# One transpose per query tile in place of two: one-hots and weight columns share a tile

## The chip, the cores and the metric

The kernel runs on one core of a Trainium2 chip. The metric is the device time of one launch in microseconds (us), taken in several runs; the median counts. One further execution is recorded by the hardware profiler, instruction by instruction. Its engines are TensorE (PE for matmuls, PEld for the loading of their stationary operand), VectorE (DVE), ScalarE (ACT), GpSimd (POOL) and the DMA queues, of which SP is the one that matters here.

## The reference

Causal attention of 8 batches, 12 heads, 448 positions and head size 64 makes an array x of 3584 tokens by 768. A gate then sends each token to one of 8 experts, and each expert keeps the 80 tokens of largest gate weight:

```python
attn = softmax(mask(q @ k.T / 8));  x = (attn @ v) as (3584, 768)
logits = x @ w_gate;  expert_idx = argmax(logits, 1)
gate_w = softmax(logits)[arange(N), expert_idx]
for e in range(8):
    tok = where(expert_idx == e)
    if len(tok) > 80: tok = the 80 of largest gate_w
    out[tok] = gate_w[tok] * (relu(x[tok] @ w1[e]) @ w2[e])   # other rows stay 0
```

## The kernel before

The program has two stages. The attention stage goes over 48 pairs of heads, six pairs to a batch. Behind it comes the expert stage, which gathers 80 tokens per expert and streams the expert weights. Between the two lies a tail, whose order is written out by hand (`TAIL`).

Each pair takes eight slots, and each engine gets its instructions in the order in which the slots issue them and executes them in that order. In the pair with number i, TensorE makes the scores of pair i + 1 at the end of slot 7, turns the probabilities of pair i - 1 in four groups of transposes (`TSLOT`: group 0 in slot 0, groups 1 and 2 in slot 1, group 3 in slot 4; tiles `tp`), and multiplies pair i - 2 with the values in slot 5 (`xp`, line 619). VectorE shifts the scores (line 558, tiles `ns`, seven shifts in slots 0, 0, 1, 2, 3, 4, 4, of widths 192, 192, 320, 320, 448, 448, 64). ScalarE takes the exponential (line 562) and copies groups 0 to 2 of the transposed probabilities to SBUF (line 601, tiles `PT`); group 3 is copied by VectorE in slot 5. Within a slot the order of issue is: group transposes, values, shifts, copies, exponential, and then the planned steps of the routing.

The routing of a batch is a list of named steps with a slot number each, counted from the end of the batch's own pairs (`STEPS`; for batch 6, the last but one, `EARLY`; batch 7, the last, takes its order from `TAIL`). Thus the steps of batch b run while the pairs of batch b + 1 are worked on, and slot 41 is slot 1 of that batch's sixth pair. The steps that matter here:

- `columns` and `parts` (GpSimd, in the last batch VectorE and GpSimd): they write one-hots of the chosen expert, three copies side by side, into the tile `oh3` (the profile calls it `oh`), and five groups of eight columns into the tile `mv`: two for the token's number and three for its gate weight, split into three bf16 parts.
- `r0t` and `r1t` (TensorE, line 864, tile `selt`): four transposes each, one per query tile of 128 tokens, of the one-hots (`r0t`) and of the weight columns (`r1t`), into a PSUM bank each.
- `r0c` and `r1c` (VectorE, line 867): copies of the 24 rows that count, to the halves 0 and 1 of the SBUF tile `ex`.
- `rl` (TensorE, line 894): reads half 0 of `ex` and compares with the table of the batches before; there is none for batch 0. `lt` (line 900) reads its result on VectorE.
- `c3w` to `c0w` (TensorE, line 878, tiles `rn`): read both halves; `c3l` to `c0l` (VectorE, line 881, `less`).

Row groups (`rt`, line 730, scaled on VectorE at line 749 into `xr`) turn the finished tokens back; in batches 0 to 5 one of them is turned in slot 40, in batch 6 one each in slots 35 and 36.

PSUM tiles of the pool `ps_g` go round through four banks in the order of issue, so a tile waits until the tile four places before it has been read. Its takers are `tp`, `selt`, `rt`, `rn`, `rl`, `xp` and some others.

Of the kernel before, what the change touches and what calls it, by code (L numbers as in the profile page):

```python
# [17 lines left out]
P = 128  # L18
# [8 lines left out]
NORMS = [0, 2, 4]  # L27
ROWS0 = [(2, 2), (3, 4), (9, 9), (19, 20)]
ROWS1 = [(27, 28), (35, 36), (36, 38), (40, 41)]
STEPS = {'gp': 20, 'gs': 22, 'lp': 24, 'lg': 25, 'logit': 26, 'shifted': 27, 'chosen': 32, 'sums': 33, 'one_hot': 33, 'columns': 33, 'weight': 35, 'weighted': 36, 'parts': 37, 'r0t': 41, 'r0c': 42, 'r1t': 42, 'r1c': 43, 'rl': 44, 'lt': 46, 'c3w': 49, 'c3l': 50, 'cp': 52, 'ro': 52, 'places': 54, 'c2w': 56, 'c2l': 57, 'places2': 54, 'c1w': 58, 'c1l': 59, 'c0w': 59, 'c0l': 60, 'earlier': 60, 'gt': 65, 'own': 67, 'rank': 67, 'rr': 68, 'tn': 73, 'tab': 74, 'rp': 76, 'row': 78}  # L30
EARLY = {'gp': 18, 'gs': 20, 'lp': 24, 'lg': 25, 'logit': 26, 'shifted': 26, 'chosen': 28, 'sums': 29, 'one_hot': 29, 'columns': 29, 'weight': 30, 'weighted': 30, 'parts': 30, 'r0t': 33, 'r0c': 34, 'r1t': 35, 'r1c': 36, 'rl': 36, 'lt': 38, 'c3w': 40, 'c3l': 41, 'c2w': 41, 'c2l': 42, 'c1w': 42, 'c1l': 43, 'cp': 43, 'ro': 43, 'c0w': 44, 'c0l': 45, 'earlier': 45, 'places': 46, 'places2': 46, 'gt': 46, 'own': 47, 'rank': 47, 'rr': 47, 'tn': 49, 'tab': 49, 'rp': 52, 'row': 53}
THIRD = [0, 0, 2, 2, 4, 6, 8]
THIRD_EARLY = [0, 2, 4, 6, 6, 8, 9]
EARLY_GATE = (2, 3)
# [138 lines left out]
def attention_then_moe(  # L173
# [12 lines left out]
    nc = tc.nc  # L186
    B, _, NP, S = qT.shape
    N, D = out.shape
    E = wg.shape[2]
# [3 lines left out]
    NT = (S + P - 1) // P  # L193
# [50 lines left out]
    SL = max(2, min(P, CAP))  # L244
    NSL = (CAP + SL - 1) // SL
    NV = 5

    COUNT = F16 if CAP + S <= 2048 else F32
    ZR = 4
# [4 lines left out]
    OFF, at = {}, 0  # L254
# [49 lines left out]
    for e, which in LAYERS:  # L304
# [4 lines left out]
        k = (K1, K2)[which - 1]  # L309
# [42 lines left out]
        return [lambda j=j, x=x: load_chunk(*got[0], j, x, 2) for j in range(k) for x in range(2)]  # L352


    mv = one_hots = mv_flat = oh_flat = expert_cols = tables = table_rows = None
# [4 lines left out]
    lg = keep.tile([P, NT, (H + 1) * E], F32, name="lg")  # L360
# [35 lines left out]
    def late_constants():  # L396


        def padded(shape, name):
            t = spool.tile(shape, BF16, name=name, tag=name, bufs=1)  # L400
            nc.gpsimd.memset(t, 0.0)
            return t
# [20 lines left out]
                                          wg_sb[j * DH:(j + 1) * DH, i:NP:2, :])  # L423

        def slots():
            nonlocal mv_flat, mv
            mv_flat = padded([P, (NT - 1) * NV * E + 2 * E + P], "mv")
            mv = mv_flat[:, 0:NT * NV * E].rearrange("k (t v e) -> k t v e", v=NV, e=E)

        def operands():  # L430
            nonlocal oh_flat, one_hots, expert_cols, tables, table_rows
            oh_flat = padded([P, (NT - 1) * 3 * E + P], "oh3")
            one_hots = oh_flat[:, 0:NT * 3 * E].rearrange("k (t v e) -> k t v e", v=3, e=E)
            expert_cols = padded([P, 2, NT * P], "ex")
            tables = [[padded([SL, 2 * E + P], f"tab{s}_{i}") for i in range(2)] for s in range(NSL)]
            table_rows = [[padded([P, SL], f"row{s}_{i}") for i in range(2)] for s in range(NSL)]
# [379 lines left out]
    def as_table(t):  # L816
        return t[:, 0:NV * E].rearrange("k (v e) -> k v e", e=E)

# [5 lines left out]
    def select_groups(bt):  # L824

        b = bt.b
        last = b == B - 1
# [25 lines left out]

            nc.gpsimd.tensor_copy(sm("held", [P, 1]), bt.rest[:, 0, 0:1])

        def expert_rows(i):
            got = []

            def turn():
                selt = bank([P, NT * P], BF16, "selt")  # L860
                got.append(selt)
                for t in range(NT):
                    src = mv_flat[:, (t * NV + 2) * E:][:, 0:P] if i else oh_flat[:, t * 3 * E:][:, 0:P]
                    nc.tensor.transpose(selt[:, t * P:(t + 1) * P], src, identb)
# [121 lines left out]
        def move(s):  # L986
# [49 lines left out]
            def row():  # L1036
# [3 lines left out]
                if s == NSL - 1:  # L1040
# [8 lines left out]
        steps = {"columns": columns, "parts": parts, "r0t": r0[0], "r0c": r0[1], "r1t": r1[0], "r1c": r1[1],  # L1049
                 "places": places, "places2": more_places, "earlier": earlier, "own": own, "rank": rank}  # L1050
        steps.update({"hold": hold, "base": base, **{f"gt{t}": lambda t=t: later_part(t) for t in range(NT)}} if last else {"gt": later})
        for t in range(NT):
# [37 lines left out]
    for b in range(B):  # L1090
        bt = Batch()
# [17 lines left out]
    def batch_plan(bt):  # L1109
# [76 lines left out]
    parts = []  # L1186
    for i, pr in enumerate(pairs):
        bt = pr.bt
# [28 lines left out]
        for k in range(SLOTS):  # L1217
# [95 lines left out]
    for i, x in enumerate(ROW_ENGINES):  # L1313
        g, t = divmod(i, NT)
# [179 lines left out]
    for s in range(NSL):  # L1494
# [14 lines left out]
        for (kind, e, *y), info in turns:  # L1509
# [5 lines left out]
            elif kind == "ld":  # L1515
                b, i, j = info
# [63 lines left out]
```

## Time and profile before

| | |
|---|---|
| median of 3 runs | 452.18 us (451.85 to 453.57) |
| profiled execution, its own time | 451.54 us |
| its span, first to last instruction | 449.8 us |
| instructions | 15801 |
| TensorE matmul busy | 427.2 us (95%) |
| VectorE busy | 384.6 us (86%) |
| ScalarE busy | 392.3 us (87%) |
| GpSimd busy | 242.8 us (54%) |

The attention stage lasts to about 310 us, the tail to about 335 us. Busy shares are averages over both stages. In the rows of a timeline the columns are start in us, duration in us, engine, line, operation, output and inputs, number of instructions merged into the row, and, in brackets, how long the engine had been idle before and what released it. A row with several instructions lasts from the start of its first to the end of its last. An instruction on VectorE or ScalarE can start a little before the visible end of the one before it.

### The profile page before, as it was taken

Reading aid. Unit: us, or ns where it says so; the run is one execution under the profiler, and the core shown is the slowest. Engines: PE = TensorE matmul, PEld = TensorE weight load, DVE = VectorE, ACT = ScalarE, POOL = GpSimd, SP = SyncE. Lnnn points to the kernel's source line nnn. Section 1 sums busy time; section 2 is a strip of 40 time slices with the busy share of each in tenths; the row PEclk is TensorE's granted clock in tenths of the full one; section 3 lists DMA queues with packets and bytes.
Section 4 is the critical chain, followed back from the end, with each engine's and each line's share of the span. In section 5 each row is a group of like instructions: output and inputs, shape, how many; then the busy total and the mean of one; then the engine's idle time right before and its main releaser. Section 6 shows DMA issues by size and latency. Waiting matters only on the chain. (4 is left out here: it accounts for less than half of the span.)

```text
span 449.8 us, 15801 instructions
## 1 busy us (share of the span) xinstructions
PE 427.2 (95%) x5830; PEld 332.1 (74%) x5830; DVE 384.6 (86%) x1315; ACT 392.3 (87%) x1069; POOL 242.8 (54%) x360
## 2 busy tenths in 40 slices
PE   7899999999999999999999999999999999999994
PEld 3566777777677777767777776766559999899993
DVE  6787788979879897987999798798879999989992
ACT  5899999989889988988998898888787999899971
POOL 7977728637664852866585185522453265415521
PEclk9899999999999999999999999999989999999999
DMA  6486748748675762866666385369989999999701
GB/s 228 123 281 210 231 162 300 223 154 282 195 237 183 236 230 82 265 211 209 222 215 221 98 264 205 106 229 383 358 283 335 406 405 396 400 414 412 310 27 45
DMA packets 47822, 109.95 MB, mean 244 GB/s; under 512 B 5970, under 2 KB 24402, under 8 KB 47104
## 3 DMA queue, kind: packets, MB, share of 16 engines
q1 hardware_dynamic: 46544, 105.20, 66.8%
q0 software_dynamic: 1056, 3.51, 2.4%
q8 instruction: 46, 0.75, 0.7%
q14 instruction: 32, 0.26, 0.2%
q10 hardware_dynamic: 144, 0.23, 0.2%
HBM read 85.35 MB, written 23.99 MB: 243 GB/s over the span
## 5 line engine op out<-in xcount | busy, mean ns | idle before, releaser
L562 ACT ACTIVATE prob<-ns,nb 128x192 f32<-128x192 f32 (+3 forms) x336 | 175.5, 532 | 18.1 <-DVE nb L558 17.4
L558 DVE CUSTOM_DVE_ANT_0 ns<-sp,mask 128x192 f32<-128x192 f32 (+3 forms) x336 | 134.5, 444 | 23.3 <-PE sp L539 21.5
L596 PE MATMUL tp<-ident,prob 128*128 128x128 f32 x768 | 104.8, 277 | 1.7 <-ACT PT L601 1.6
L1157 DVE SCALAR_TENSOR_TENSOR wl<-wraw,wh 128x768 f16<-128x768 f32 (+1 forms) x99 | 98.4, 1065 | 1.7 <-issue 1.6
L487 POOL TENSOR_TENSOR qk<-qk,qk 128x448 f16<-128x448 f32 x94 | 96.3, 1040 | 4.5 <-DVE qk L515 1.3
L619 PE MATMUL xp<-PT,vt 128*64 128x448 f32 (+3 forms) x768 | 93.6, 386 | 2.8 <-DVE xr L749 2.4
L1151 ACT ACTIVATE wh<-wraw 128x768 f16<-128x768 f32 (+1 forms) x99 | 86.5, 934 | 7.2 <-PE hp L1445 4.5
L596 PEld LDWEIGHTS tp<-ident,prob 128*128 128x128 f32 x768 | 84.6, 141 | 4.7 <-ACT PT L601 3.4
L619 PEld LDWEIGHTS xp<-PT,vt 128*64 128x64 f32 x768 | 50.9, 136 | 46.6 <-issue 24.7
L601 ACT COPY PT<-tp 128x512 f32<-128x512 f32 x144 | 76.2, 589 | 8.5 <-PE tp L596 8.0
L539 PE MATMUL sp<-qk 64*128 64x448 f16 (+2 forms) x864 | 69.1, 300 | 3.9 <-POOL qk L487 2.8
L1444 PEld LDWEIGHTS <-wh 128*128 128x128 f16 x678 | 68.2, 101 | 1.1 <-issue 1.1
L1445 PEld LDWEIGHTS <-wh 128*128 128x128 f16 x678 | 67.7, 100 | 1.3 <-issue 1.2
L1446 PEld LDWEIGHTS <-wl 128*128 128x128 f16 x678 | 67.7, 100 | 0.6 <-issue 0.6
L562 ACT ACTIVATION_READ_ACCUMULATOR prob<-ns,nb 128x1 f32 x336 | 66.4, 198 | 0.0
L1490 POOL DMA_INDIRECT out<-yo,idx x8 | 36.4, 4549 | 51.7 <-ACT yo L1487 47.5
L539 PEld LDWEIGHTS <-qk 64*128 64x128 f16 x864 | 36.8, 95 | 18.8 <-issue 3.1
L601 DVE COPY PT<-tp 64x256 f32<-64x256 f32 x144 | 43.6, 328 | 2.3
L1445 PE MATMUL hp<-xl,wh 128*128 128x80 f16 x336 | 37.8, 202 | 0.8 <-issue 0.8
L1444 PE MATMUL hp<-xh,wh 128*128 128x80 f16 x336 | 37.9, 202 | 0.0
L1446 PE MATMUL hp<-xh,wl 128*128 128x80 f16 x336 | 37.8, 202 | 0.0
L1444 PE MATMUL op<-hh,wh 128*128 128x80 f16 x318 | 36.3, 202 | 0.6 <-issue 0.6
(187 smaller groups left out, 660.7 us busy)
## 6 DMA issues: line engine op xcount, KB each, us to landing
wraw<-w SPq DMA_DIRECT2D x49, 384.0 KB, 9.5
wraw<-w SPq DMA_DIRECT2D x29, 512.0 KB, 9.3
out<-mask SPq DMA_DIRECT2D x56, 192.0 KB, 2.1
qk<-k_t SPq DMA_DIRECT2D x23, 448.0 KB, 3.3
qk<-q_t SPq DMA_DIRECT2D x23, 448.0 KB
vt<-v_t SPq DMA_DIRECT2D x24, 384.0 KB, 5.3
xs<-xr SPq DMA_DIRECT2D x42, 192.0 KB, 4.7
wraw<-w SPq DMA_DIRECT2D x24, 256.0 KB, 3.7
```

The costliest lines, as they stand in the source:

```text
L487: sub = lambda e, o, a, b: e.tensor_tensor(out=o, in0=a, in1=b, op=ALU.subtract)
L539: nc.tensor.matmul(pr.sp[t, j], a[rows, p, queries(t)], c[rows, p, FROM[t]:FROM[t] + WIDTH[t]], start=(x == 0), stop=(x == 2))
L558: nc.vector.tensor_tensor_reduce(out=ns, in0=pr.sp[x], in1=m, scale=-1.0 / 8.0, scalar=HUGE, op0=ALU.add, op1=ALU.min, accum_out=nb)
L562: nc.scalar.activation(pr.P[:, OFF[x]:OFF[x] + w], got[0], AF.Exp, bias=got[1], scale=-1.0, accum_out=pr.sums[:, h:h + 1])
L596: nc.tensor.transpose(tp[:, i * P:(i + 1) * P], f, ident)
L601: way(part_of(pr.PT, rows, to, *todims), part_of(got[0], rows, at, *dims))
L619: nc.tensor.matmul(xp[rows, c * P:S], st["vt"][:, c, p * P + j * DH:p * P + (j + 1) * DH], pr.PT[:, j, n0:n0 + w], start=(c == 0), stop=(c ...
L1151: nc.scalar.activation(hi_of[y][:, 0:src.shape[1]], src, AF.Copy, scale=SW)
L1157: nc.vector.scalar_tensor_tensor(out=lo_of[y][:, 0:n], in0=src, scalar=SW, in1=hi_of[y][:, 0:n], op0=ALU.mult, op1=ALU.subtract)
L1444: nc.tensor.matmul(o, wh[:, ws], h[:, c, :], start=begin, stop=False, skip_group_check=True)
L1445: nc.tensor.matmul(o, wh[:, ws], l[:, c, :], start=False, stop=False, skip_group_check=True)
L1446: nc.tensor.matmul(o, wl[:, ws], h[:, c, :], start=False, stop=end, skip_group_check=True)
```

## The change

One-hots and weight columns move into one tile, `columns`, with a block of 96 columns per query tile: the `mv` columns at 16 to 55 of the block, so that the weights begin at 32, and the one-hots at 64 to 87. In batches 0 to 6 one transpose of 128 columns per query tile turns the whole block: the weights come out in rows 32 to 55 of the PSUM tile and the one-hots in rows 64 to 87. Step `r1t` is gone. The two copies read from one bank, at partitions 64 and 32, and still write to partition 0. The slots change too: `r0t` goes from 41 to 42 and `r0c` from 42 to 43, where `r1c` stays (batch 6: `r0t` from 33 to 34, `r0c` from 34 to 35, `r1c` stays at 36). The last batch keeps two sets of transposes and their order; its first reads 32 columns per query tile, starting at the one-hots, and its second 128, starting at the weights.

```diff
-STEPS = {..., 'r0t': 41, 'r0c': 42, 'r1t': 42, 'r1c': 43, 'rl': 44, ...}
-EARLY = {..., 'r0t': 33, 'r0c': 34, 'r1t': 35, 'r1c': 36, 'rl': 36, ...}
+STEPS = {..., 'r0t': 42, 'r0c': 43, 'r1c': 43, 'rl': 44, ...}
+EARLY = {..., 'r0t': 34, 'r0c': 35, 'r1c': 36, 'rl': 36, ...}
...
+    CM, CO, CW = 32, 64, 96
+    assert 3 * E <= 32 and 2 * E <= CM
...
         def slots():
-            nonlocal mv_flat, mv
-            mv_flat = padded([P, (NT - 1) * NV * E + 2 * E + P], "mv")
-            mv = mv_flat[:, 0:NT * NV * E].rearrange("k (t v e) -> k t v e", v=NV, e=E)
+            nonlocal columns_of, one_hots, mv
+            columns_of = padded([P, (NT - 1) * CW + CM + P], "columns")
+            blocks = columns_of[:, 0:NT * CW].rearrange("k (t c) -> k t c", c=CW)
+            mv = blocks[:, :, CM - 2 * E:CM - 2 * E + NV * E].rearrange("k t (v e) -> k t v e", e=E)
+            one_hots = blocks[:, :, CO:CO + 3 * E].rearrange("k t (v e) -> k t v e", e=E)
...
-            oh_flat = padded([P, (NT - 1) * 3 * E + P], "oh3")
-            one_hots = oh_flat[:, 0:NT * 3 * E].rearrange("k (t v e) -> k t v e", v=3, e=E)
...
-        def expert_rows(i):
+        def expert_rows(*which):
             got = []
+            at = [CO, CM]
 
             def turn():
                 selt = bank([P, NT * P], BF16, "selt")
                 got.append(selt)
+                w = 32 if which == (0,) else P
                 for t in range(NT):
-                    src = mv_flat[:, (t * NV + 2) * E:][:, 0:P] if i else oh_flat[:, t * 3 * E:][:, 0:P]
-                    nc.tensor.transpose(selt[:, t * P:(t + 1) * P], src, identb)
-
-            def copy():
-                (nc.scalar.copy if last else nc.vector.tensor_copy)(bt.ex[0:3 * E, i], got[0][0:3 * E])
-            return [turn, copy]
-
+                    c = t * CW + (at[which[0]] if last else 0)
+                    nc.tensor.transpose(selt[0:w, t * P:(t + 1) * P], columns_of[:, c:c + w], identb)
+
+            def copy(i):
+                r = 0 if last else at[i]
+                (nc.scalar.copy if last else nc.vector.tensor_copy)(bt.ex[0:3 * E, i], got[0][r:r + 3 * E])
+            return [turn] + [lambda i=i: copy(i) for i in which]
...
-        r0, r1 = expert_rows(0), expert_rows(1)
+        rows = expert_rows(0) + expert_rows(1) if last else expert_rows(0, 1)
```

## Rows read from the trace of the kernel before

**Rows 1.** Table of stretches: busy time and instructions of PE, PEld, DVE, ACT, POOL

```profile
110.00:160.00 50.00, 48.76 (x547) 35.49 (x547) 43.98 (x194) 44.39 (x143) 31.98 (x54) 1.00 0.65 208
```

**Rows 2.** Timeline of batch 1 around the two sets of transposes, all engines

```profile
108.31 0.24 POOL L849 TENSOR_TENSOR mv<-grest,mv 128x32 bf16<-128x32 f32 x1
...
108.55 1.08 ACT L601 COPY PT<-tp 128x512 f32<-128x512 f32 x2 [0.18 <-PE tp L596]
...
108.68 0.32 PEld L864 LDWEIGHTS <-oh 128*128 128x128 bf16 x4
...
108.96 0.27 PEld L864 LDWEIGHTS <-mv 128*128 128x128 bf16 x4
109.00 0.08 DVE L558 DVE_READ_ACCUMULATOR2_ANT nb<- 128x1 f32 x1
...
109.19 0.42 PEld L596 LDWEIGHTS tp<-ident,prob 128*128 128x128 f32 x4
109.21 0.41 DVE L867 COPY ex<-selt 24x512 bf16<-24x512 bf16 x1
...
109.55 0.60 DVE L558 CUSTOM_DVE_ANT_0 ns<-sp,mask 128x448 f32<-128x448 f32 x1
...
109.68 0.18 PEld L894 LDWEIGHTS <-ex 128*128 128x128 bf16 x4
...
109.93 0.20 PEld L619 LDWEIGHTS xp<-PT,vt 128*64 128x64 f32 x4
...
110.09 0.41 DVE L867 COPY ex<-selt 24x512 bf16<-24x512 bf16 x1
...
113.21 1.30 PEld L596 LDWEIGHTS tp<-ident,prob 128*128 128x128 f32 x12
...
113.91 1.56 ACT L601 COPY PT<-tp 128x512 f32<-128x512 f32 x3
```

**Rows 3.** Timeline of VectorE: copy from partitions 64 up, then two from 0

```profile
150.11 0.43 DVE L601 COPY PT<-tp 64x256 f32<-64x256 f32 x1
...
150.55 0.48 DVE L601 COPY PT<-tp 64x128 f32<-64x128 f32 x2
```

**Rows 4.** Timeline of batch 2, the pair behind `rl`

```profile
153.89 0.75 DVE L881 SCALAR_TENSOR_TENSOR less<-rn,ggw,before 128x512 bf16<-128x512 f32 x1 [0.60 <-PE rn L878]
...
155.68 0.20 PEld L619 LDWEIGHTS xp<-PT,vt 128*64 128x64 f32 x4 [0.57 <-DVE xr L749]
```

**Rows 5.** Timeline of batch 0, ScalarE in the pair behind the transposes

```profile
75.83 0.19 ACT L562 ACTIVATION_READ_ACCUMULATOR prob<-ns,nb 128x1 f32 x1
...
76.11 1.57 ACT L601 COPY PT<-tp 128x512 f32<-128x512 f32 x3
```

**Rows 6.** Timeline of batch 6 (`EARLY`) around the two sets of transposes

```profile
297.07 0.32 PEld L864 LDWEIGHTS <-oh 128*128 128x128 bf16 x4
...
298.04 0.24 POOL L849 TENSOR_TENSOR mv<-grest,mv 128x32 bf16<-128x32 f32 x1
298.08 0.60 DVE L558 CUSTOM_DVE_ANT_0 ns<-sp,mask 128x448 f32<-128x448 f32 x1
298.34 0.24 PEld L864 LDWEIGHTS <-mv 128*128 128x128 bf16 x4
...
299.31 0.54 DVE L749 TENSOR_TENSOR xr<-rt,sums 128x384 f32<-128x384 f32 x1
...
299.78 0.40 DVE L867 COPY ex<-selt 24x512 bf16<-24x512 bf16 x1
...
300.23 0.20 PEld L619 LDWEIGHTS xp<-PT,vt 128*64 128x64 f32 x4 [0.16 <-DVE ex L867]
...
303.09 0.36 DVE L558 CUSTOM_DVE_ANT_0 ns<-sp,mask 128x192 f32<-128x192 f32 x1 [0.61 <-PE sp L539]
```

**Rows 7.** Timeline of the tail: the last batch's first transposes, and GpSimd

```profile
321.56 0.40 PE L864 MATMUL selt<-identb,oh 128*128 128x128 bf16 x4 [0.38 <-DVE oh L835]
...
321.59 0.24 POOL L838 TENSOR_TENSOR mv<-goh,pnum 128x32 bf16<-128x32 f32 x1
```

More of the change, by code (lines that the diff above doesn't have):

```diff
@@ L29 @@
 ROWS1 = [(27, 28), (35, 36), (36, 38), (40, 41)]
-STEPS = {'gp': 20, 'gs': 22, 'lp': 24, 'lg': 25, 'logit': 26, 'shifted': 27, 'chosen': 32, 'sums': 33, 'one_hot': 33, 'columns': 33, 'weight': 35, 'weighted': 36, 'parts': 37, 'r0t': 41, 'r0c': 42, 'r1t': 42, 'r1c': 43, 'rl': 44, 'lt': 46, 'c3w': 49, 'c3l': 50, 'cp': 52, 'ro': 52, 'places': 54, 'c2w': 56, 'c2l': 57, 'places2': 54, 'c1w': 58, 'c1l': 59, 'c0w': 59, 'c0l': 60, 'earlier': 60, 'gt': 65, 'own': 67, 'rank': 67, 'rr': 68, 'tn': 73, 'tab': 74, 'rp': 76, 'row': 78}
-EARLY = {'gp': 18, 'gs': 20, 'lp': 24, 'lg': 25, 'logit': 26, 'shifted': 26, 'chosen': 28, 'sums': 29, 'one_hot': 29, 'columns': 29, 'weight': 30, 'weighted': 30, 'parts': 30, 'r0t': 33, 'r0c': 34, 'r1t': 35, 'r1c': 36, 'rl': 36, 'lt': 38, 'c3w': 40, 'c3l': 41, 'c2w': 41, 'c2l': 42, 'c1w': 42, 'c1l': 43, 'cp': 43, 'ro': 43, 'c0w': 44, 'c0l': 45, 'earlier': 45, 'places': 46, 'places2': 46, 'gt': 46, 'own': 47, 'rank': 47, 'rr': 47, 'tn': 49, 'tab': 49, 'rp': 52, 'row': 53}
+STEPS = {'gp': 20, 'gs': 22, 'lp': 24, 'lg': 25, 'logit': 26, 'shifted': 27, 'chosen': 32, 'sums': 33, 'one_hot': 33, 'columns': 33, 'weight': 35, 'weighted': 36, 'parts': 37, 'r0t': 42, 'r0c': 43, 'r1c': 43, 'rl': 44, 'lt': 46, 'c3w': 49, 'c3l': 50, 'cp': 52, 'ro': 52, 'places': 54, 'c2w': 56, 'c2l': 57, 'places2': 54, 'c1w': 58, 'c1l': 59, 'c0w': 59, 'c0l': 60, 'earlier': 60, 'gt': 65, 'own': 67, 'rank': 67, 'rr': 68, 'tn': 73, 'tab': 74, 'rp': 76, 'row': 78}
+EARLY = {'gp': 18, 'gs': 20, 'lp': 24, 'lg': 25, 'logit': 26, 'shifted': 26, 'chosen': 28, 'sums': 29, 'one_hot': 29, 'columns': 29, 'weight': 30, 'weighted': 30, 'parts': 30, 'r0t': 34, 'r0c': 35, 'r1c': 36, 'rl': 36, 'lt': 38, 'c3w': 40, 'c3l': 41, 'c2w': 41, 'c2l': 42, 'c1w': 42, 'c1l': 43, 'cp': 43, 'ro': 43, 'c0w': 44, 'c0l': 45, 'earlier': 45, 'places': 46, 'places2': 46, 'gt': 46, 'own': 47, 'rank': 47, 'rr': 47, 'tn': 49, 'tab': 49, 'rp': 52, 'row': 53}
 THIRD = [0, 0, 2, 2, 4, 6, 8]
@@ L352, in piece_parts @@
         return [lambda j=j, x=x: load_chunk(*got[0], j, x, 2) for j in range(k) for x in range(2)]
-    mv = one_hots = mv_flat = oh_flat = expert_cols = tables = table_rows = None
+    mv = one_hots = columns_of = expert_cols = tables = table_rows = None
     identb = before = dec = number = number_after = pnum = tbase = wgd = slots_e = slots_t = None
@@ L425, in slots @@
         def slots():
-            nonlocal mv_flat, mv
-            mv_flat = padded([P, (NT - 1) * NV * E + 2 * E + P], "mv")
-            mv = mv_flat[:, 0:NT * NV * E].rearrange("k (t v e) -> k t v e", v=NV, e=E)
+            nonlocal columns_of, one_hots, mv
[3 more added lines that the diff above has]
+            one_hots = blocks[:, :, CO:CO + 3 * E].rearrange("k t (v e) -> k t v e", e=E)
         def operands():
-            nonlocal oh_flat, one_hots, expert_cols, tables, table_rows
-            oh_flat = padded([P, (NT - 1) * 3 * E + P], "oh3")
-            one_hots = oh_flat[:, 0:NT * 3 * E].rearrange("k (t v e) -> k t v e", v=3, e=E)
+            nonlocal expert_cols, tables, table_rows
             expert_cols = padded([P, 2, NT * P], "ex")
@@ L1048, in select_groups @@
         moves = [f for s in range(NSL) for f in move(s)]
-        steps = {"columns": columns, "parts": parts, "r0t": r0[0], "r0c": r0[1], "r1t": r1[0], "r1c": r1[1],
+        steps = {"columns": columns, "parts": parts, **dict(zip(("r0t", "r0c", "r1t", "r1c") if last else ("r0t", "r0c", "r1c"), rows)),
                  "places": places, "places2": more_places, "earlier": earlier, "own": own, "rank": rank}
```

## Prediction

> **What bounds the kernel now.** I read the table of stretches first, because the change lies in the attention stage, which fills the first 310 us. In a middle stretch of 50 us TensorE is busy for 48.8, ScalarE for 44.4, VectorE for 44.0 and GpSimd for 32.0 [rows 1]. No engine is simply full: three engines hand one pair of heads to each other, and what counts is which hand-over ends last. So I went to the timeline around the edited steps. The groups of lines and the table of waits give sums over all batches; which of two ends came last can be read from the timeline alone.
>
> The timeline of batch 1 [rows 2] shows how tight the place is. I call the four transposes of the one-hots A, the four of the weight columns B, their copies to SBUF a and b, the score shifts on VectorE x0 to x6 and the groups of probability transposes g0 to g3. TensorE runs g0, one row group, g1 and g2, then A at 108.68, B at 108.96, g3 at 109.19, rl at 109.68 (it reads the copied one-hot rows) and the values product xp at 109.93. VectorE runs copy a at 109.21, between x3 and x4, and copy b at 110.09, behind x4. Copy a ends at 109.62 and rl begins at 109.68. ScalarE's copies of g1 and g2, which start at 108.55 and last 1.08, end at 109.63. So the end of g3, the end of ScalarE's copies and the end of copy a fall together within 0.1 us: rl has no slack against any of them.
>
> Then I asked whether xp is on the path that sets the pace. The next twelve transposes start at 113.21, ScalarE's copies of them follow at 113.91, 0.70 behind [rows 2]. In the same place of batch 2, VectorE's comparison is waiting 0.60 us for TensorE, and the next xp waits 0.57 us for VectorE [rows 4]. A later xp therefore makes everything behind it later, on all three engines, and nothing takes it back. This pattern is the same in batches 1 to 5.
>
> **The change, part by part.** Removed: B in seven batches. A takes 108.96 - 108.68 = 0.28 us of TensorE and B 109.19 - 108.96 = 0.23 [rows 2]; the merged transposes cost as much as A, so TensorE has 0.23 us less to do per batch, 1.6 us in all. One PSUM bank less is taken as well. The four banks go round, so g3 no longer takes the bank that ScalarE frees half-way through its two copies at 108.55 to 109.63, but that of the row group before it. g3 can start at 108.96.
>
> Moved: copy a goes from slot 42 to slot 43. A slot's score shift is issued ahead of its planned steps, so copy a now stands behind x4 and not ahead of it. What TensorE has saved it then spends waiting at rl, which is next in its queue behind g3, with xp behind rl. The sum for batches 1 to 5: x4 can start when x3's accumulator is read, at 109.00, and keeps VectorE for 110.09 - 109.55 = 0.54 [rows 2], so until 109.54. Copy a then runs to 109.95 (0.41), and rl follows 0.05 later, at 110.00 instead of 109.68: 0.32 us later.
>
> To this comes a cost of the new source rows. The merged transpose leaves the weights at partitions 32 to 55 and the one-hots at 64 to 87, while shifts read from partition 0. Where VectorE goes from a copy that reads partitions 64 and up to copies that read from 0, the second starts 0.44 us behind a first of 0.43, not before its end [rows 3]; copy a, of 0.41, let x4 start after 0.34 [rows 2]. So a change of the start partition costs about 0.08. I charge it three times a batch (x4 to a, a to b, b to x5); only the first lies ahead of rl, which makes 0.40 us for xp. The bounds are 0.32 (no such cost) and 0.48 (twice). The other two fall where VectorE has more room: copy a's own wait for A, about 0.1 us between 109.00 and 109.21, is gone. The Trainium skill, "VectorE: DVE Perf Modes", section "Two Vector instructions with no wait between them", says the same as a rule: an instruction whose start quadrant of 32 partitions differs from that of the last one that read the same memory is held until all earlier ones have finished. By it all three starts are held; without it batches 1 to 5 would lose 1.6 us in place of 2.0. The trace agrees where it can show it, with 0.44 behind 0.43.
>
> The merged transposes also need the weights, which GpSimd writes last at 108.31 + 0.24 = 108.55, against a start at 108.68 [rows 2]. That is covered by 0.13 us, and a delay of up to 0.4 would still not reach copy a at its new place, so I count nothing. Batches 1 to 5: 5 x 0.40 = 2.0 us.
>
> Batch 6 has its own table (EARLY), and there the cover is gone. A stands at 297.07, B at 298.34, and GpSimd's last weight write ends at 298.04 + 0.24 = 298.28 [rows 6]. The merged transposes stand at A's place in the queue, ahead of a row group, and must wait there for the weights: TensorE stands still from 297.07 to 298.34. Copy a follows A's start by 109.21 - 108.68 = 0.53 [rows 2], so it runs from 298.87 to 299.28. Behind x4 (298.08 + 0.54 = 298.62) the next shift was free to go; now it starts at 299.28, 0.66 later. The row group's scaling goes from 299.31 to 299.97 and copy b from 299.78 to 300.44, with the change of partition 300.52, to end at 300.92. In the new round of four banks rl takes the bank that b frees (a merged tile is free only after both copies): 300.97, and xp 0.25 later, as 109.93 is behind 109.68: 301.22 instead of 300.23. That is 1.0 us. Behind it VectorE's first shift already waits 0.61 for TensorE [rows 6], so it passes on in full. Bounds: 0.3, if only the bank and one copy delay it, and 1.3, the whole stall.
>
> Batch 0 has no rl. There TensorE gains up to 0.23, but ScalarE ends its accumulator read at 76.02 and starts the next copies at 76.11 [rows 5], so it can take only 0.1 of it. Bounds 0 and 0.23.
>
> The last batch keeps its eight transposes. Its first four read 32 columns only, and start at 321.56, when VectorE has written the one-hots. GpSimd's products for neighbouring columns end at 321.59 + 0.24 = 321.83 [rows 7]. If the shared tile made the transposes wait for them it would cost 0.3; the columns read don't overlap those written, so I take 0. Wider steps in the writes of a few dozen elements and one memset in place of two at the start I count at nothing: GpSimd has 18 us of 50 free [rows 1].
>
> Sum: 2.0 + 1.0 - 0.1 = 2.9 us longer. The profiled execution took 451.54 us (span 449.8), so 454.4; the median of the runs is 452.18, 0.64 above it, so 455.1.
>
> **The rivals.** First, the saving comes through: VectorE does copy a before rl needs it, and TensorE is 0.23 us ahead in seven batches, 1.6 us, with 450.6 as the time. It decides if copy a ends by about 109.4, which is the end of g3 when it starts at 108.96. For it speaks that TensorE has the highest busy share [rows 1]; against it that x4's 0.54 us and the copy's 0.41 don't fit between 109.00 and 109.4. Second, the waits are there but half of their price is taken up in the next pairs, by idle time like the 0.57 in front of xp [rows 4]: 1.0 to 1.9 us, so 453.2 to 454.1. Against it: that idle time is itself a wait for work that starts from the late TensorE. Third, copies that read from partitions 32 and 64 are slower than 0.41, or the last batch waits for GpSimd too: with 0.2 more in each of six batches and 0.3 at the end it is 1.5 us more, 456.6. No row of before shows such a copy of 24 partitions; the 64-partition one at 0.43 for 256 elements [rows 3] gives no sign of it.
>
> **How the numbers follow.** My forecast 0.63, the saving 0.08, half taken up 0.20, the dearer one 0.09. About 0.5% (2.3 us) is what a measurement here can tell from no change. Of the forecast about 0.05 lies below 454.4 and counts as the same, with all of the half-price case and most of the saving: 0.31; slower 0.67; faster 0.02. The forecast's own range comes from its bounds, 5 x 0.32 + 0.3 - 0.2 = 1.7 and 5 x 0.48 + 1.3 = 3.7, so 453.9 to 455.9; for 8 in 10 it reaches into the half-price case and to the dearer one: 452.9 to 456.6.
>
> **What the profile after would show.** Right: a pair of copies side by side behind x4, an rl whose TensorE waits about 0.6 us behind an earlier g3, and an interval from selt's start to xp of 1.65 in place of 1.25 us in batches 1 to 5; a stall of 1.2 us in front of the merged transposes in batch 6. From one batch to the next the pace would be 0.4 us slower. Wrong: xp earlier than 1.25 us behind selt, copies longer than 0.45 us, a period that doesn't grow although xp is late, or a longer stretch between 320 and 335 us.

## The result, and the profile after

The changed kernel takes 458.01 us in the median of 4 runs (454.17 to 459.34), the kernel before 452.02 in the runs beside it: a ratio of 1.0111, 95% interval 1.0080 to 1.0143. It is slower, as forecast, but by 6.0 us and not by 2.9, and outside the range of 452.9 to 456.6. The profiled execution took 456.83 us with a span of 455.1. The four runs lie wide apart and go with the granted clock of TensorE, averaged over the run: 454.17 us at 0.998, 456.83 at 0.992, 459.20 and 459.34 at 0.986. A run over 1.5% above the fastest of its kernel counts in the medians given here and not in the ratios.

The place that the prediction worked out first, batch 1, in the timeline of the changed kernel (start, duration, engine, line, what; the line numbers are 2 to 4 higher than before):

```profile
107.29 0.32 PEld L868 LDWEIGHTS <-columns 128*128 128x128 bf16 x4
107.40 0.39 PE L868 MATMUL selt<-identb,columns 128*128 128x128 bf16 x4
107.61 0.61 DVE L560 CUSTOM_DVE_ANT_0 ns<-sp,mask 128x448 f32<-128x448 f32 x1
108.26 0.86 DVE L872 COPY ex<-selt 24x512 bf16<-24x512 bf16 x2
108.73 0.19 PEld L898 LDWEIGHTS <-ex 128*128 128x128 bf16 x4 [0.74 <-DVE ex L872]
108.98 0.20 PEld L621 LDWEIGHTS xp<-PT,vt 128*64 128x64 f32 x4
```

The two copies stand side by side behind the shift x4, and `rl` has waited 0.74 us for the first of them, with `xp` behind it. From the weight load of the transposes to that of `xp` it takes 108.98 - 107.29 = 1.69 us, where it took 109.93 - 108.68 = 1.25 [rows 2]. In batch 6 the merged transposes wait for GpSimd's weights, and `xp` goes 0.05 us behind copy b, whose bank it takes:

```profile
299.08 0.23 PEld L868 LDWEIGHTS <-columns 128*128 128x128 bf16 x4 [1.22 <-POOL columns L851]
299.52 0.42 DVE L872 COPY ex<-selt 24x512 bf16<-24x512 bf16 x1 [0.42 <-PE selt L868]
299.97 0.62 DVE L560 CUSTOM_DVE_ANT_0 ns<-sp,mask 128x448 f32<-128x448 f32 x1
301.24 0.42 DVE L872 COPY ex<-selt 24x512 bf16<-24x512 bf16 x1
301.26 0.30 PE L898 MATMUL rl<-row,ex 128*128 128x80 bf16 x4 [0.69 <-DVE xr L751]
301.71 0.20 PEld L621 LDWEIGHTS xp<-PT,vt 128*64 128x64 f32 x4 [0.28 <-DVE ex L872]
```

What each batch costs is read from the start of `xp` in the pair with the transposes, the same pair in both traces:

| `xp` at the edited place of batch | before | after | difference | this batch's share |
|---|---|---|---|---|
| the pairs ahead of batch 0's | 47.53 | 46.37 | -1.16 | |
| 0 (next pairs) | 84.66 | 83.27 | -1.39 | -0.23 |
| 1 | 109.93 | 108.98 | -0.95 | +0.44 |
| 2 | 148.82 | 148.30 | -0.52 | +0.43 |
| 3 | 187.71 | 187.62 | -0.09 | +0.43 |
| 4 | 226.60 | 226.94 | +0.34 | +0.43 |
| 5 | 265.50 | 266.26 | +0.76 | +0.42 |
| 6 | 300.23 | 301.71 | +1.48 | +0.72 |
| last `xp` of the stage | 315.19 | 316.66 | +1.47 | 0 |

The -1.16 at the top is not the change's: it arises at the start of the program and comes out anywhere between -1.4 and +0.5 in the traces below, so only differences of differences are used. The change costs the attention stage 1.47 + 1.16 = 2.6 us. That leaves 3.4 of the 6.0 us. From the last `xp` to the end of the span it is 449.8 - 315.19 = 134.6 us before and 455.1 - 316.66 = 138.4 after. The routing in the tail keeps about this distance (the first gather is issued 1.34 us later); what is lost lies behind it, in the hand-over to the experts. Its timeline before (25 idle matmuls `wp` keep TensorE busy, SP issues the experts' weights, GpSimd the first gather of tokens, `xtp` turns the gathered tokens):

```profile
329.28 6.32 PE L1312 MATMUL wp<-before,identb 128*128 128x448 bf16 x25
330.65 1.64 SPq L334 DMA_DIRECT2D wraw<-w  x1
330.66 1.07 POOL L1357 DMA_INDIRECT xg<-xs,idx  x1 [4.17 <-DMA out<-mask]
333.14 0.33 SPq L334 DMA_DIRECT2D wraw<-w  x1
335.44 0.58 PE L1373 MATMUL xtp<-ident,xg 80*128 80x80 f32 x6
```

and after:

```profile
330.64 4.89 PE L1316 MATMUL wp<-before,identb 128*128 128x448 bf16 x25
332.00 1.08 POOL L1361 DMA_INDIRECT xg<-xs,idx  x1 [4.04 <-DMA out<-mask]
332.13 0.41 SPq L336 DMA_DIRECT2D wraw<-w  x1
332.64 0.40 SPq L336 DMA_DIRECT2D wraw<-w  x1
338.64 0.87 PE L1377 MATMUL xtp<-ident,xg 80*128 80x80 f32 x6 [3.12 <-DMA xg<-xs,idx]
```

Before, `xtp` follows the idle matmuls with no wait, 4.78 us behind the gather's issue. After, it comes 6.64 us behind it and TensorE has stood still for 3.12 us. SP has issued two weight loads within 0.65 us of the gather; before, its first issue lasted 1.64 us and the second came 2.5 us later. The table of stretches shows what follows (columns as in [rows 1]; the third number from the end is the granted clock as a share of 2.4 GHz). Of before:

```profile
329.00:332.00 3.00, 3.00 (x12) 1.44 (x13) 0.85 (x6) 3.00 (x4) 1.19 (x2) 0.50 0.98 339
335.00:350.00 15.00, 15.00 (x299) 14.51 (x296) 15.00 (x18) 10.37 (x17) 5.68 (x3) 1.00 1.03 347
```

Of after:

```profile
335.00:338.60 3.60, 0.53 (x3) 0.08 (x1) 3.60 (x4) 1.04 (x2) 2.26 (x2) 1.00 1.00 343
338.60:342.20 3.60, 3.56 (x18) 3.01 (x18) 2.33 (x4) 0.70 (x2) 0.96 (x1) 0.53 1.03 307
335.00:350.00 15.00, 11.88 (x180) 10.90 (x179) 12.70 (x15) 7.21 (x14) 4.18 (x4) 0.89 1.01 328
```

Between 327 and 350 us TensorE's clock falls to its lower level of 1.2 GHz once in both. Before, that happens at 329 to 332 us, for the most part in matmuls whose result nobody reads. After, it happens behind the idle 3 us, in the experts' first products. Wait and clock, with the 1.3 us by which the routing is later, leave 180 matmuls from 335 to 350 us in place of 299.

What moved in place of the gather shows in the view of the DMA queues for 332 to 333 us (q1 is SP's queue, q0 that of the gathers, q8 carries instruction code; packets, MB, share of 16 engines). Of before, in which SP's second load has not come yet:

```profile
DMA packets 80, 0.07 MB, mean 67 GB/s; under 512 B 53, under 2 KB 72, under 8 KB 80
q1 hardware_dynamic: 25, 0.05, 20.9%
q0 software_dynamic: 55, 0.02, 10.5%
```

Of after:

```profile
DMA packets 266, 0.36 MB, mean 361 GB/s; under 512 B 31, under 2 KB 266, under 8 KB 266
q1 hardware_dynamic: 266, 0.36, 102.1%
```

The gather's first packets move between 332.25 and 332.5 us before, 1.6 us or more behind its issue, and after 335.5 us in the changed kernel, 3.5 us behind it. One thing more differs: before, a block of instruction code is loaded between 330 and 331 us,

```profile
q8 instruction: 1, 0.02, 9.9%
```

after, none is between 322.5 and 342 us. The whole page counts 46 such blocks, 0.75 MB, before and 45 after. Before has 5830 matmuls, each with a weight load, so 11660 instructions of TensorE, 253 to a block; they come every 6 us in the experts' stage, where TensorE works through some 130 matmuls in that time. In the other traces, too, the page counts 46 blocks where TensorE has 5830 matmuls or more, and 45 where it has 5814 or fewer. So I take these for TensorE's blocks. The change takes 28 transposes, 56 instructions, out of TensorE's program ahead of the tail, and the block that used to be crossed in the idle matmuls is crossed behind the first `xtp`.

### The profile page after: what moved, and what is told of

It reads as the page before. It is cut to its first block, busy times and chain, and to the rows that moved or that the text cites. A ratio compares the mean times of both kernels' runs of the same rounds, so it can differ in the third digit from the quotient of the medians.

```text
span 455.1 us, 15745 instructions
## 1 busy us (share of the span) xinstructions
PE 425.7 (94%) x5802; PEld 330.7 (73%) x5802; DVE 385.9 (85%) x1315; ACT 392.1 (86%) x1069; POOL 236.6 (52%) x359
## 4 chain that ended last, share of the span: by engine, by line
PE 60%; DVE 7%; DMA 5%; ACT 4%; issue 2%; POOL 2%; SPq 1%; POOLq 0%; DVEq 0%; ACTq 0%
PE xp L621 12%; PE tp L598 10%; PE sp L541 7%; DMA vt<-v_t 3%; PE hp L1449 3%; PE hp L1450 3%; PE hp L1448 3%; ACT PT L603 3%; PE rt L732 3%; PE op L1448 3%; PE hp L1445 3%; PE op L1450 3%; PE op L1449 3%; DVE ns L560 2%; PE gp L682 2%
## 5 line engine op out<-in xcount | busy, mean ns | idle before, releaser
L1494 POOL DMA_INDIRECT out<-yo,idx x8 | 34.9, 4362 | 53.9 <-ACT yo L1491 42.9
L1450 PE MATMUL op<-hh,wl 128*128 128x80 f16 x318 | 36.4, 202 | 0.6 <-issue 0.6
```

What stands on the lines that cost most here:

```text
L1450: nc.tensor.matmul(o, wl[:, ws], h[:, c, :], start=False, stop=end, skip_group_check=True)
```

## The experiments

**Theory.** Two losses that have nothing to do with each other: in the attention stage the new order (copy a behind x4, and batch 6's stall), 2.6 us; in the hand-over the place of a code block, by which the weight loads get ahead of the first gather, 3.4 us. **Rival.** The merged tile or later routing itself upsets the hand-over. The first run asks how far the kernel before spreads by itself, the next three ask about the attention stage.

**before_again**, the kernel before unchanged.

> The kernel before, unchanged, to see what its own executions differ by and at which granted clock. If the change alone makes the time spread (454 to 459 us), these stay within 451.5 to 454 us. If the spread comes from chance in the hand-over to the experts, which any program can meet, some of these reach 455 us or more.

452.07 us (12 runs, 450.46 to 452.74), ratio 1.0001 (0.9984 to 1.0018). The spread of the changed kernel is not met here.

**slots_back**: the changed kernel, with transposes and copy a at their old slots in batches 0 to 5; batch 6 stays as changed.

```diff
-STEPS = {..., 'r0t': 42, 'r0c': 43, 'r1c': 43, ...}
+STEPS = {..., 'r0t': 41, 'r0c': 42, 'r1c': 43, ...}
```

> The merged transposes with the slots of before in batches 0 to 5 (transposes in 41, first copy in 42, second in 43); batch 6 as changed. Theory of the queue position: the first copy stands ahead of the 448-wide shift again, the interval from the transposes to the values product falls from 1.68 to about 1.25 us in batches 1 to 5, and the stretch from the values product of the ninth pair to the last one shrinks by 5 x 0.44 = 2.2 us, from 251.66 to about 249.5 us. Rival, that the copies from partitions 64 and 32 are what costs: nothing changes, 251.7 us. For the whole time: 2.2 us less than the changed kernel if the loss before the experts passes on in full; no change beyond its spread if what decides lies in the hand-over.

**batch6_two**: the changed kernel, with two sets of transposes at their old slots in batch 6 as in the last batch.

```diff
-EARLY = {..., 'r0t': 34, 'r0c': 35, 'r1c': 36, 'rl': 36, ...}
+EARLY = {..., 'r0t': 33, 'r0c': 34, 'r1t': 35, 'r1c': 36, 'rl': 36, ...}
...
+            two = b >= B - 2
...
-                    c = t * CW + (at[which[0]] if last else 0)
+                    c = t * CW + (at[which[0]] if two else 0)
...
-        rows = expert_rows(0) + expert_rows(1) if last else expert_rows(0, 1)
+        rows = expert_rows(0) + expert_rows(1) if b >= B - 2 else expert_rows(0, 1)
```

> The changed kernel, but batch 6 keeps its two sets of transposes, its two banks and its old slots, as the last batch does. Theory: the 1 us stall of TensorE for GpSimd's weight columns is gone, the stretch from the ninth pair's values product to the last shrinks by 0.73 us, from 251.66 to 250.9. Rival, that batch 6 loses its time by the later first copy and the bank alone: the stall is gone but the stretch shrinks by less than 0.3 us.

**rl_behind_xp**: batch6_two, with `rl` a slot later in batches 1 to 5, so that `xp` no longer stands behind it.

```diff
-STEPS = {..., 'rl': 44, ...}
+STEPS = {..., 'rl': 45, ...}
```

> Merged transposes and the late slots in batches 0 to 5, batch 6 with two sets, and the table product rl moved from slot 44 to 45, behind the values product. Theory that rl's wait is what holds up the values product: it starts about 0.9 us behind the transposes (1.68 in the changed kernel, 1.25 before), the scores start about 0.1 us earlier than before in each batch, and the stretch from the ninth pair's values product to the last is 248.0 to 249.0 us (before 249.03, changed 251.66). Rival, that the bank round or VectorE's later shifts set the pace: 250.5 us or more. Whole time: 451 to 452 us if the loss ahead of the experts explains the change, 454 to 459 us if the hand-over to the experts does.

In the attention stage, all three did what the theory said (difference of `xp` to the kernel before; ahead of batch 0, behind batch 5, last):

| | ahead | behind 5 | last | stage's cost | whole, us | ratio |
|---|---|---|---|---|---|---|
| after | -1.16 | +0.76 | +1.47 | +2.6 | 458.01 | 1.0111 (1.0080 to 1.0143) |
| slots_back | -0.05 | -0.25 | +0.48 | +0.5 | 457.33 | 1.0125 (1.0094 to 1.0156) |
| batch6_two | -0.42 | +1.54 | +1.52 | +1.9 | 458.75 | 1.0137 (1.0102 to 1.0173) |
| rl_behind_xp | -0.04 | -0.93 | -0.95 | -0.9 | 454.49 | 1.0048 (1.0026 to 1.0070) |

With the old slots batches 1 to 5 lose nothing (and win nothing, though B is gone there too), with two sets batch 6 loses nothing, and with `rl` behind `xp` each batch brings 0.14 us. But the whole did not follow: slots_back, which should have taken back 2.1 us, is no faster, and rl_behind_xp is slower than before with a shorter attention stage. In all three `xtp` waits for the gather, 2.93, 4.03 and 3.19 us.

**slots_only**: the kernel before, only with A and copy a one slot later; the layout and the number of instructions stay.

```diff
-STEPS = {..., 'r0t': 41, 'r0c': 42, 'r1t': 42, 'r1c': 43, ...}
+STEPS = {..., 'r0t': 42, 'r0c': 43, 'r1t': 42, 'r1c': 43, ...}
```

> The kernel before, with only the order of the change: each query tile keeps two transposes and two tiles, but transposes A and copy a stand one slot later, where the change puts them, so both transposes and then both copies come together. TensorE runs as many instructions as before. Theory of the attention stage (copies behind the shift x4 delay the values product): batches 1 to 5 lose 0.3 to 0.45 us each, the last values product starts 1.5 to 2.2 us later than before. Theory of the hand-over (its loss comes with the 56 instructions that TensorE has no longer): the first gather lands in 4 to 5 us as before, the first expert transposes do not wait for it, and the whole is 453.5 to 454.5 us. Rival (any delay of the attention stage upsets the hand-over): the first expert transposes wait some 3 us for the gather, and the whole is 456 to 458 us.

453.94 us, ratio 1.0035 (1.0018 to 1.0052). Batches 1 to 5 lose 0.32 us each (the difference goes from +0.14 ahead of them to +1.73 behind). A block is loaded at 332.0 us, SP's issue beside it, here the last write of `out`, lasts 2.04 us, and the first `xtp` does not wait. A later attention stage alone does not make the first gather late.

**after_rows** and **rl_rows**: after and rl_behind_xp, with small idle matmuls added at the start until TensorE's instruction count is that of before.

```diff
-    for _ in range(9):
-        nc.tensor.matmul(idle, corners[0][:, 0, 0, :], corners[0].rearrange("k x p q -> k (x p q)"), ...)
+    for i in range(37):   # rl_rows: 33, two of them wide
+        n = 512 if i < 1 else 64
+        nc.tensor.matmul(idle[0:128, 0:n], corners[0][:, 0, 0, 0:128], corners[0]...[:, 0:n], ...)
```

> The changed kernel, with 28 more idle matrix multiplications at the start (1 of 512 columns and 36 of 64 in place of 9 of 512), which bring the count of TensorE's instructions ahead of the tail back to that of before (56 more rows). Theory (the loss of the hand-over comes with the place at which a block of TensorE's instructions is loaded, and with nothing of the merged tile): the first gather lands in 4 to 5 us, the first expert transposes do not wait, and of the loss only that of the attention stage is left, 2.6 us: 454 to 455 us. Rival (the loss of the hand-over belongs to the merged tile, its memory layout or the later routing): the first expert transposes wait some 3 us, the whole is 457 to 458.5 us.

> The version with logits' operand behind the values product and two sets in batch 6, whose attention stage was 0.93 us faster than before, with 24 more idle matrix multiplications at the start (2 of 512 columns and 31 of 64 in place of 9 of 512), 48 rows more, so that TensorE has the instruction count of before. Theory of the code blocks: the hand-over goes as before, and the whole is 450.6 to 451.8 us, faster than both kernels. Rival (merged tile): 454 to 455 us, as without the rows.

Both missed: 459.28 us, ratio 1.0120 (1.0079 to 1.0161), and 454.69, ratio 1.0040 (1.0011 to 1.0068). But neither had done what it was meant to: their blocks came at 342.75 and 339.25 us, still behind the first `xtp`. A count of all matmuls up to a block, taken from the table of stretches, shows how near it was: the block ahead of the hand-over is loaded when 3404 have begun before and 3403 in after_rows, and the 25 idle ones begin with the 3493rd in both. The next block comes at the 3496th before, among the idle ones, and at the 3533rd in after_rows, behind the first `xtp`. From one block to the next the count runs from 61 to 208, so it does not tell where exactly a block is asked for.

**before_rows200**: the kernel before, with 100 more small idle matmuls at the start (1 of 512 columns and 108 of 32 in place of 9 of 512), which are to move the block out of the hand-over.

> The kernel before, computing just the same, with 100 more small idle matrix multiplications at the start (1 of 512 columns and 108 of 32 in place of 9 of 512), 200 rows more; with blocks of 256 rows TensorE's code then stands to the blocks as in the changed kernel, which has 56 fewer. Theory of the code blocks: with no change of the routing at all the first expert transposes wait some 3 us for the gather, TensorE's granted clock falls in the first matrix multiplications of the experts, and the whole is 455 to 458 us (the start may add or take up to 1 us, to be read from the first values product). Rival (merged tile or the later routing): no wait, 451.5 to 453 us beside that of the start.

With no change of the routing, no block came between 320.25 and 340.0 us, SP issued two weight loads within 0.5 us of the gather, and `xtp` had to wait:

```profile
329.57 1.07 POOL L1358 DMA_INDIRECT xg<-xs,idx  x1 [4.17 <-DMA out<-mask]
329.58 0.39 SPq L335 DMA_DIRECT2D wraw<-w  x1
330.06 0.40 SPq L335 DMA_DIRECT2D wraw<-w  x1
336.17 0.64 PE L1374 MATMUL xtp<-ident,xg 80*128 80x80 f32 x6 [1.61 <-DMA xg<-xs,idx]
```

So that half held without the merged tile. The price did not: 452.99 us, ratio 1.0027 (1.0004 to 1.0050), not 455 to 458. In the trace the clock fell in the idle matmuls (they took 6.37 us), so the wait was shorter and the experts ran at full clock. But the traced execution, 450.38 us, is the fastest of the twelve, which reach 455.80; six lie above 453.5, at a mean granted clock of 0.983 to 0.990 in place of 0.995. What happened in those no trace shows.

**after_rows90**: the changed kernel with 45 more idle matmuls at the start, 17 beyond after_rows.

```diff
-    for _ in range(9):
+    for i in range(54):   # one of 512 columns, 53 of 64
```

> The changed kernel with 45 more idle matrix multiplications at the start (1 of 512 columns and 53 of 64 in place of 9 of 512). The runs so far show a 16 KB block of the instruction queue at the hand-over (330.3, 329.5 and 332.0 us) in the three kernels whose first gather lands in time, and none there in those where it lands late; with 28 more matrix multiplications the block still came behind the first expert transposes (342.8 us). Counted in TensorE's matrix multiplications up to the block, 45 more should put it among the 25 idle ones of the hand-over. Theory (the block's load delays the weights and lets the gather pass): a block at 329 to 332 us, an issue of SP over 1 us long, the first expert transposes with under 0.5 us of wait, no fall of the granted clock in the experts' first products, and 454 to 455 us. Rival (the block is a bystander; the merged routing itself delays the gather): a block at the hand-over, but the wait of 3 us stays, and 457 to 459 us.

454.47 us, ratio 1.0065 (1.0038 to 1.0092). By the medians that is 3.5 us less than the changed kernel, and 2.6 more than before, which is the attention stage's loss (in this trace 3.09 - 0.44 = 2.65). By the ratios it is 0.46% or 2.1 us less, and the two intervals just overlap; nine of the twelve runs lie at 453.1 to 455.3 us, three at 458.9 to 461.2. The block is at 333.5 us, SP's issue is long, and the gather lands 3.85 us behind its issue:

```profile
333.64 1.07 POOL L1362 DMA_INDIRECT xg<-xs,idx  x1 [4.05 <-DMA out<-mask]
333.75 1.57 SPq L337 DMA_DIRECT2D wraw<-w  x1
335.42 0.38 SPq L337 DMA_DIRECT2D wraw<-w  x1
337.49 0.61 PE L1378 MATMUL xtp<-ident,xg 80*128 80x80 f32 x6 [0.34 <-DMA xg<-xs,idx]
```

**after_warm**: the changed kernel with 37 in place of 25 idle matmuls at the hand-over.

```diff
-gt1 c0l gt0 earlier own *5 rank rr tn tab *25
+gt1 c0l gt0 earlier own *5 rank rr tn tab *37
```

> The changed kernel with 37 in place of 25 idle matrix multiplications ahead of the first expert transposes, some 3 us more of work that nobody reads. The gather lands as late as in the changed kernel (6 to 7 us after its issue), but TensorE is not idle meanwhile. Theory (half of the hand-over's loss is the granted clock, which falls after the idle 3 us and halves the speed of the experts' first products): the granted clock falls during the idle products, not in the experts', the second expert transposes come some 1.5 to 2 us sooner behind the first than in the changed kernel (6.2 us), and the whole is 455.5 to 456.5 us. Rival (only the wait for the gather counts, the clock's fall is hidden elsewhere): 457.5 to 458.5 us.

455.92 us, ratio 1.0083 (1.0059 to 1.0107). The gather is as late as ever, 7.1 us, but in the trace the clock stays up and the second `xtp` follows 4.52 us behind the first, as before; in the changed kernel it was 6.17. By the medians some 2 us of the hand-over's loss were the clock. The interval overlaps that of the changed kernel, and the traced execution, 453.64 us, is the second fastest of twelve, so the size is not shown.

```profile
330.56 7.16 PE L1316 MATMUL wp<-before,identb 128*128 128x448 bf16 x37
339.05 0.61 PE L1377 MATMUL xtp<-ident,xg 80*128 80x80 f32 x6 [1.33 <-DMA xg<-xs,idx]
343.57 0.61 PE L1377 MATMUL xtp<-ident,xg 80*128 80x80 f32 x6
335.00:350.00 15.00, 13.67 (x227) 11.87 (x226) 13.51 (x16) 7.72 (x15) 4.89 (x4) 1.00 1.02 333
```

**after_fence** and **rl_fence**: after and rl_behind_xp, with SP held by hand until the first gather is issued.

```diff
             if u.e == 0:
                 nc.gpsimd.memset(split_bufs["lo"][0][:, 0:1], 0.0)
+                nc.gpsimd.memset(fence[:, 0:16], 0.0)
+                nc.sync.dma_start(fence[:, 16:32], fence[:, 0:16])
```

> The changed kernel, in which SP's weight loads of the hand-over are held until GpSimd has issued the first gather: GpSimd writes a small tile right behind it, and a transfer of SP that reads this tile stands ahead of the loads. Theory (the gather is late because the weights were queued ahead of it): SP's first weight load starts some 1.5 us later, the gather lands in 4 to 5 us in place of 6.5, the first expert transposes wait under 1.5 us in place of 3.1, the granted clock does not fall in the experts' products, and the whole is 454 to 455.5 us, which is the attention stage's loss of 2.6 us and at most 1 more. Rival (the gather is slow by itself, or the weights that come later cost as much): 457 to 459 us.

> The version whose attention stage is 0.93 us faster than before, with the same hold of SP's weight loads behind the first gather. Theory: its hand-over is as that of before, within 1 us: 451 to 452.2 us, 0 to 1 us faster than the kernel before. Rival: 454 to 455 us as without the hold.

The gather landed within 5.0 and 3.5 us and the first `xtp` did not wait, though no block was near (324.75 and 344.0; 337.0): holding back the weights is enough to bring the gather in time.

```profile
333.20 1.07 POOL L1362 DMA_INDIRECT xg<-xs,idx  x1 [4.05 <-DMA out<-mask]
334.45 0.71 SPq L1513 DMA_DIRECT2D fence<-fence  x1
335.26 0.35 SPq L336 DMA_DIRECT2D wraw<-w  x1
338.24 0.58 PE L1378 MATMUL xtp<-ident,xg 80*128 80x80 f32 x6
```

The medians came down by 1 to 2 us only, to 456.85 us, ratio 1.0102 (1.0070 to 1.0134), and 452.68, ratio 1.0020 (0.9997 to 1.0044), and both intervals overlap those without the hold. Both times lie above what was expected. The weights now start 2.1 us behind the gather, and in after_fence the third `xtp` comes 14.4 us behind the second, before 12.5. So the theory's own price for the hold, at most 1 us, was probably too small.

**rl_rows90**: rl_behind_xp with 45 more idle matmuls, both losses removed.

> The version whose attention stage is 0.93 us faster than before (logits' operand behind the values product, two sets in batch 6), with 45 more idle matrix multiplications at the start, so that the block of TensorE's instructions is loaded at the hand-over, as in the changed kernel with these 45. Theory (attention stage and hand-over are two separate losses that add up, and nothing else is lost): a block between 326 and 332 us, the first expert transposes with under 0.5 us of wait, and 450.8 to 451.8 us, 0.3 to 1.2 us faster than the kernel before. Rival (the merged routing loses something in the experts' stage besides): 453 us or more.

451.57 us against 452.37 of the kernel before beside it, ratio 0.9989 (0.9965 to 1.0013). The block is at 327.75, 1.9 us ahead of the gather, and the wait 0.77 us, not under 0.5. The median is where the sum of the two theories puts it, and 2.9 us below rl_behind_xp; here the intervals (1.0026 to 1.0070 there) do not overlap. A shift of the program's start is not behind it: ahead of batch 0, `xp` differs from the kernel before by -0.01 us here and by -0.04 in rl_behind_xp. That it is faster than before is within the interval and not shown. Its trace still has a fall of the clock in the experts' products (0.89 over 335 to 350 us).

**onehots_low**: the changed kernel, with the one-hots in columns 0 to 23 of a block and the weights in 64 to 87.

```diff
-    CM, CO, CW = 32, 64, 96
+    CM, CO, CW = 64, 0, 96
```

> The changed kernel with the one-hots in columns 0 to 23 and the weights in columns 64 to 87 of each block, so that copy a reads from partition 0, as the shifts around it do, and copy b alone from another. Theory (VectorE holds an instruction that starts at another partition until the one before has ended): copy a starts about 0.1 us sooner behind the shift x4, and batches 1 to 5 lose 0.32 to 0.36 us each at the values product in place of 0.44. Rival (no such hold): 0.44 each as before. The hand-over, and so the whole, is not what it is run for.

Batches 1 to 5 lose 0.31 to 0.33 us each, as in slots_only; the whole was 454.70 us in one execution. Copy a starts 0.54 us behind x4, in the changed kernel 0.65:

```profile
107.40 0.61 DVE L560 CUSTOM_DVE_ANT_0 ns<-sp,mask 128x448 f32<-128x448 f32 x1
107.94 0.86 DVE L872 COPY ex<-selt 24x512 bf16<-24x512 bf16 x2
```

All traces side by side, one execution each. Block: the time against the gather's issue of a block loaded up to 2 us ahead of it or, where there is none, of the next one behind; tail: last `xp` to the end of the span; clock: mean granted share from 335 to 350 us.

| | block, us | gather's issue to `xtp` | wait of `xtp` | clock | tail |
|---|---|---|---|---|---|
| before | -0.4 | 4.8 | 0 | 1.00 | 134.6 |
| before_again | -0.5 | 4.9 | 0 | 1.00 | 135.1 |
| slots_only | -0.4 | 4.7 | 0 | 1.00 | 136.2 |
| after_rows90 | -0.1 | 3.9 | 0.34 | 1.00 | 134.7 |
| rl_rows90 | -1.9 | 4.3 | 0.77 | 0.89 | 136.4 |
| before_rows200 | +10.4 | 6.6 | 1.61 | 1.00 | 134.6 |
| after_warm | +10.6 | 7.1 | 1.33 | 1.00 | 135.3 |
| rl_fence | +8.6 | 3.5 | 0 | 1.00 | 137.0 |
| after_fence | +10.8 | 5.0 | 0 | 0.98 | 138.3 |
| onehots_low | +10.1 | 6.4 | 2.37 | 0.89 | 137.2 |
| after | +10.3 | 6.6 | 3.12 | 0.89 | 138.4 |
| slots_back | +10.3 | 7.8 | 2.93 | 0.89 | 138.2 |
| rl_rows | +10.8 | 6.6 | 2.05 | 0.77 | 140.3 |
| rl_behind_xp | +12.2 | 6.7 | 3.19 | 0.66 | 140.6 |
| after_rows | +10.9 | 7.8 | 4.23 | 0.66 | 141.5 |
| batch6_two | +10.7 | 8.2 | 4.03 | 0.66 | 141.8 |

Apart from the two with a hold, the gather is in time where a block is loaded just ahead of its issue and late where none is. The tail goes with the clock more than with the wait: it is 134.6 to 137.0 us at 1.00 and over 140 below 0.8 (after_fence, whose weights were late, stands apart).

## Why the prediction was half right

The attention stage as a whole was forecast at +2.9 us and measured at +2.6; the whole kernel at +2.9 and +6.0.

**Batches 1 to 5: right.** Predicted 0.40 each, measured 0.42 to 0.44; from the transposes to `xp` 1.65 us predicted, 1.69 measured. Its two terms can be told apart: the order alone costs 0.32 (slots_only, onehots_low), as worked out from x4's 0.54 and the copy's 0.41; the change of the start partition costs 0.11 and not 0.08. The Trainium skill ("VectorE: DVE Perf Modes", section "Two Vector instructions with no wait between them") says that an instruction whose start quadrant (a group of 32 partitions) differs from that of the last reader of the same memory is held until every earlier one has finished. The traces agree: with the one-hots at partition 64, copy a starts 0.04 us behind the end of x4, at partition 0 it starts 0.07 us ahead of it and so 0.11 us sooner.

**Batch 6: right mechanism, size off.** Predicted 1.0, measured 0.72. The stall is there (1.22 us for GpSimd's weights), and copy b starts within 0.05 us of the time predicted. The term that failed is "rl takes the bank that b frees": `rl` went ahead while copy b ran, let go by the row group's scaling (`xr`), and `xp` took that bank, so 0.27 us less.

**Batch 0: predicted -0.1, measured -0.23.** ScalarE's short gap behind its accumulator read did not stop the gain.

**Half taken up, the saving, dearer copies.** None came: the shares of the five batches are equal and add up, and a copy takes 0.415 to 0.419 us.

**The step that failed** is the sum, "2.0 + 1.0 - 0.1 = 2.9 us longer", set on the time of the whole kernel: it ends with the attention stage and puts what lies behind at nothing. The term for the last batch, "I take 0", holds for its transposes, but there is no term for the hand-over behind them. The prediction named "a longer stretch between 320 and 335 us" as a sign of being wrong and put no price on it; the loss came for the most part just behind, from 335.5 to 343 us. There the change cost 3.4 us by the medians and 138.4 - 134.6 = 3.8 in the two traces: it left TensorE's program 56 instructions shorter, a code block was no longer loaded beside SP's first weight loads, these got ahead of the first gather, TensorE stood still for 3 us and the experts' first products ran at half clock. That the place of the code and not the merged tile decides is shown by idle matmuls at the start alone: 45 of them bring back 3.5 us by the medians in after_rows90, where the remaining 2.6 are the attention stage's, and 2.9 us in rl_rows90, with intervals clear of each other; 28 and 24, which leave the block behind the first `xtp`, bring back nothing (after_rows, rl_rows).

**What stays open.** Why a block beside SP's issue goes with a long one: four of the five traces with a block there show it (1.64, 1.11, 2.04 and 1.57 us; of rl_rows90 the records of SP around the block are missing), which is a coincidence in time and no proof of the way. What decides where the clock falls is open as well: in the trace of before_rows200 the fall came in the idle matmuls, in those of most merged kernels without a block in the experts' products. With it the price of a late gather stays open. One run of the changed kernel, at a mean clock of 0.998, took 454.17 us, only 2.1 us above the kernel before, which leaves nothing for the hand-over; the price varies from run to run, and whether the gather was late in that run no trace shows.

## What to carry to other kernels

A sum over the edited stage is not a sum over the kernel: follow the order in which two queues reach a shared resource at the next hand-over, and give it a term of its own even if the change does not touch it. Where an engine in order feeds another one, a step removed is worth nothing if the operand of the next one has been moved later in the other's queue; here a slot of 0.32 us was lost to win 0.23, and with the old slots the removed step won nothing in batches 1 to 5 (slots_back), where `rl` then waits 0.30 us for copy a in place of it. And before a difference of 1% is put down to an idea, the same program with a few idle instructions more is worth a run: it moved this kernel by 2 to 3.5 us.

## What was not expected of the hardware

The place of a block of instruction code moved the time by 0.5 to 0.8% (after and after_rows90, rl_behind_xp and rl_rows90; ratios and medians). The Trainium skill ("Runtime: NRT & Kernel Launch", section "Instruction fetch mechanics") says that a sequencer loads its code in blocks of 16 KiB through a queue of its own while it executes, at a cost that is mostly hidden. The trace agrees with the blocks (46, 0.75 MB, one to 253 instructions) but the kernel is faster with the block in the hand-over than without, by 2.9 us in the medians of rl_behind_xp and rl_rows90, so its side effect is not small, and here the measurement decides.

A gather on GpSimd's queue got no packets through for 3.5 us behind its issue in the changed kernel, with q1 at 102% of the engines from 332 to 333 us, and 55 of them from 332 to 333 us in the kernel before, with q1 at 21%. A full queue of SP is not the whole reason: in the half microseconds from 335.5 to 337.5 us the gather's packets pass beside q1 at 87 to 112%. Whether they were held back or came late themselves is not shown.
